# Turning the step's result on VectorE: 32x32 blocks out of PSUM in place of two TensorE transposes

## The chip, the cores and the metric

The kernel runs on one core of one Trainium2 chip. Times are device microseconds (us) of that core. A profiled execution gives a span (first to last instruction) and a trace, and its own time is a little longer than the span.

## The reference, cut to what matters

Two independent layers are put side by side. Layer B is a long convolution; the change touches none of its arithmetic. Layer A is an attention that carries a small memory from one segment of 32 rows to the next, 64 segments (steps) in sequence:

```python
for s in range(n_seg):                                   # 64 steps
    h = concatenate([mem, x[s*32:(s+1)*32]])             # 8 memory rows + 32 rows, 1024 columns
    q, k, v = h @ Wq, h @ Wk, h @ Wv                     # 1024 -> 32 heads x 128
    p = softmax(where(mask, q @ k.T * 128**-0.5, -1e9))
    o = (p @ v) @ Wo                                     # back to 1024 columns
    mem = o[:8]                                          # the only link to the next step
    outs.append(o[8:])
```

So a step can't begin its projections of the memory rows before the step in front has its result `o`. All weights together are 32 MB in bfloat16, and not all of them stay on chip.

## The kernel before, in words

The first 700 us or so hold layer B and, woven into it, what of layer A does not depend on the memory: x is transposed (`Ahead.transposes`, L93), and the keys and queries (`PKd`) and values (`VXd`) of eight rows of each segment are computed ahead and parked in DRAM (`Ahead.projections`, L115). Then `part_a` (L233) runs the 64 steps one after another, under an order of instructions that is written out by hand: each engine executes its instructions in the order of the program text, and only semaphores tie the engines together.

One step, from L478 on. `hT` is the step's input, already transposed: 128 partitions, 8 chunks of the 1024 columns (`kc`, called keys here when a chunk of a weight is meant), 32 columns, of which 24 are x rows (`XM`) and the last 8 the memory rows. `quads` (L358) does one projection of 16 heads: for each of the eight keys `kc` four matmuls, one for each quarter of TensorE's columns, with `hT[:, kc, :]` as stationary operand. The step goes: k of half 0, q of half 0, part of k of half 1, transposes of k and q (`tr`), scores of half 0 (`scores`, L387), and so on through q, v, softmax, and the output projection (`oproj`, L468), which sums into `pp[:, 1, :]` in PSUM: 128 partitions x 256 float32, where partition 32*qt+r holds row r and columns 256*qt to 256*qt+255.

Weights come from three places. Most stay on chip. Twelve of the 64 blocks of a step (512 KB each) are streamed from DRAM copies `WD` into four rotating buffers `wst`; the SP queue issues a load (`stage`, L294) as soon as TensorE has finished with the buffer. Three blocks are kept in PSUM (`KEPT`, L29) and are copied by VectorE into a shared scratch tile just before use: `fetch` (L311) makes five copies (L292) for key 7 of k, whose last piece goes to the tile `a_S`.

The scratch tile `arena` is one block of bytes with hand-given places (`AT`, L36). The place `ob` (byte 4960, 1024 bytes) holds the step's result on its way out; the place `pk` (byte 0) holds the parked keys and queries of the step. `load_pk` (L325) is issued on ScalarE's queue; `put_kl` (L378) is GpSimd's copy (L379) from it into the tile `KT0`, which the first score matmul (L390) needs.

The end of a step before the change, L564 to L584, in the order of each engine:

- TensorE: the output projection; the five small matmuls for `pl` (L444, L448); two 128x128 transposes of the result, `tro` (L574); then key 0 of the next step.
- ScalarE: two copies of `pp[:, 1]` to `osb`, the first half of `ob` (L568); copy L579; the issue of `load_pk` for the next step (L581, its trace line is L327); copy L582; the issues of two stores (L343, L347).
- VectorE: two copies from `tro` into the memory columns of `hT` (L576); then the five copies of `fetch`.

The first projection of a step takes its keys in the order 0, 2, 4, 6, 1, 3, 5, 7, because the first L576 fills the even chunks and the second the odd ones. The GpSimd copy `put_xt` (L336) has filled the x columns of `hT` long before.

Of the kernel before, what the change touches and what calls it, by code (L numbers as in the profile page):

```python
# [10 lines left out]
BF16 = mybir.dt.bfloat16  # L11
F32 = mybir.dt.float32
# [27 lines left out]


def weight_blocks(Wq, Wk, Wv, Wo):
    W3 = {"k": Wk.rearrange("(kc p) he -> kc p he", p=128),
          "q": Wq.rearrange("(kc p) he -> kc p he", p=128),
          "v": Wv.rearrange("(kc p) he -> kc p he", p=128)}
    WoU = Wo.rearrange("(u h e) d -> u e h d", h=2, e=128)

    def src(key):
        if isinstance(key, str):
            return W3[key]  # L50
        if key[0] == "o":
            return WoU[key[1]]
        m, t, kc = key
        return W3[m][kc][:, t * 2048:(t + 1) * 2048]
    return src
# [18 lines left out]
class Ahead:  # L74
# [18 lines left out]
    def transposes(self, pool, ps, ident):  # L93
        nc = self.nc
        def load(b):
            xb = pool.tile([128, self.Dm], BF16, name="xb", tag="xb")
            nc.gpsimd.dma_start(out=xb[:], in_=self.x[b * 128:(b + 1) * 128, :])
            return xb
        xbs = [load(b) for b in range(3)]
        yield  # L100
        for b in range(self.S // 128):
            if b + 3 < self.S // 128:
                xbs.append(load(b + 3))
            xb = xbs[b]
            pt = ps.tile([128, self.KC, 4, self.SL], BF16, name="pt_x", tag="ptx")
            for kc in range(self.KC):
                nc.tensor.transpose(out=pt[:, kc, :, :].rearrange("p a b -> p (a b)"), in_=xb[:, kc * 128:(kc + 1) * 128], identity=ident[:])
            yield
            xst = pool.tile([128, 4, self.KC, self.XM], BF16, name="xst", tag="xst")
            nc.scalar.copy(out=xst[:].rearrange("p s k r -> p k s r"), in_=pt[:, :, :, 0:self.XM])  # L110
            nc.scalar.copy(out=self.xTl[:, :, 4 * b:4 * b + 4, :], in_=pt[:, :, :, self.XM:self.SL])  # L111
            nc.sync.dma_start(out=self.VXd[4 * b:4 * b + 4, :, 256:].rearrange("s p f -> p s f"), in_=xst[:].rearrange("p s k r -> p s (k r)"))
            yield
# [119 lines left out]
def part_a(ctx, tc, x, src, WD, HE, seg_len, out_a, ahead, W_res, rest, places, first):  # L233
    nc = tc.nc
    S, Dm = x.shape
    M = 8
    SL = seg_len
    E = 128
    KC = Dm // 128
    NS = S // SL  # L240
    assert SL == 32 and M == 8 and Dm == 1024 and HE == 4096
    XM = 24
# [114 lines left out]
    for s in range(NS):  # L357
        def quads(m, t, kcs, a=None):  # L358
            if a is None:
                a = ps.tile([128, 512], F32, name="acc", tag=BANK[m, t])  # L360
            for kc in kcs:
                w = unit((m, t, kc))
                for g in range(4):
                    for o_, rhs in columns(w, 512 * g, 512):
                        nc.tensor.matmul(a[32 * g:32 * g + 32, o_:o_ + rhs.shape[1]], lhsT=hT[:, kc, :], rhs=rhs,  # L365
                                         start=(kc == 0), stop=(kc == KC - 1), tile_position=(0, 32 * g), skip_group_check=True)
            return a
# [107 lines left out]
                            nc.tensor.matmul(po[32 * qt:32 * qt + 32, o_:o_ + rhs.shape[1]], lhsT=oT[:, h % 4, (h % 16) // 4, :], rhs=rhs,  # L475
                                             start=False, stop=(h == 31), tile_position=(0, 32 * qt), skip_group_check=True)

        a = quads("k", 0, (0, 2, 4, 6, 1, 3, 5, 7))  # L478
        k0 = evac(a, "k0")
        a = quads("q", 0, range(0, 6))  # L480
        fetch(("q", 0, 7))
# [82 lines left out]
        oproj(pp[:, 1, :], (8, 10, 12, 14, 9, 11, 13, 15), o1)  # L564
        ob = at("ob", 2, 256)
        osb = ob[:, 0, :]
        for j in range(2):
            nc.scalar.copy(out=osb[:, 128 * j:128 * j + 128], in_=pp[:, 1, 128 * j:128 * j + 128])  # L568
        pl = ps.tile([128, 4, 32], F32, name="pl", tag="b2")
        pv_l(pl[:], 1, V1, L1)  # L570
        if s + 1 < NS:
            pt_o = [ps.tile([128, 4, SL], BF16, name="tro", tag=tag) for tag in ("b0", "b1")]
            for j in range(2):
                nc.tensor.transpose(out=pt_o[j][:].rearrange("p a b -> p (a b)"), in_=osb[:, 128 * j:128 * j + 128], identity=ident[:])  # L574
            for j in range(2):
                nc.vector.tensor_copy(out=hT[:, :, XM:SL].rearrange("p (q j) r -> p j q r", j=2)[:, j], in_=pt_o[j][:, :, XM:SL])  # L576
        if s + 1 < NS:
            fetch(("k", 0, 7))
        nc.scalar.copy(out=ob[:, 1, 0:128], in_=pp[:, 0, 0:128])  # L579
# [815 lines left out]
@with_exitstack  # L1395
def kernel(
    ctx: ExitStack,
    tc: tile.TileContext,
    A_x: bass.AP,
    A_mem0: bass.AP,  # L1400
    A_Wq: bass.AP,
    A_Wk: bass.AP,
    A_Wv: bass.AP,
    A_Wo: bass.AP,
    A_seg_len: bass.AP,
    B_u: bass.AP,
    B_A_re: bass.AP,
    B_A_im: bass.AP,
    B_B_re: bass.AP,
    B_B_im: bass.AP,  # L1410
    B_C_re: bass.AP,
    B_C_im: bass.AP,
    B_log_dt: bass.AP,
    B_Dskip: bass.AP,
    out: bass.AP,
):
    seg_len = int(A_seg_len)
    Dm = A_x.shape[2]
    Db = B_u.shape[2]
    out_a = out[0, :, 0:Dm]  # L1420
    out_b = out[0, :, Dm:Dm + Db]
    src = weight_blocks(A_Wq.rearrange("d h e -> d (h e)"), A_Wk.rearrange("d h e -> d (h e)"),
                        A_Wv.rearrange("d h e -> d (h e)"), A_Wo.rearrange("h e d -> (h e) d"))
    WD, copies = streamed_copies(ctx, tc, src)
    ahead = Ahead(ctx, tc, A_x[0], src, seg_len)
    ctx_w = ctx.enter_context(ExitStack())
    W_res, places, first = {}, [], {}
    rest = Keys(RESIDENT)
    rest.ctx = ahead.ctx = ctx_w

    def residents(stay, early):
        def put(t_):
            load_resident(tc, None, src, rest.pop(0), W_res, None, t_)
        for _ in range(EARLY[0]):
            load_resident(tc, stay, src, rest.pop(0), W_res)
            yield
        four = ahead.pool.tile([128, 4, 2048], BF16, name="W4", tag="kst")
        for t_ in [four[:, i, :] for i in range(4)]:
            put(t_)
            yield  # L1440
        for n in range(2):
            for t_ in early[0:6] if n == 0 else early[6:8]:
                put(t_)
                yield
            two = stay.tile([128, 2, 2048], BF16, name="W2", tag="KT%d" % n)
            for i in range(2):
                put(two[:, i, :])
                yield
        two = ahead.pool.tile([128, 2, 2048], BF16, name="W2", tag="xTl")
        for i in range(2):  # L1450
            put(two[:, i, :])
            yield
        for _ in range(4):
            put(ahead.pool.tile([128, 2048], BF16, name="W1", tag="wsl", bufs=4))
            yield
        ahead.wst = ctx_w.enter_context(tc.tile_pool(name="a_wst", bufs=1, side="right"))
        pool = ctx_w.enter_context(tc.tile_pool(name="a_wre0", bufs=1, side="right"))
        for _ in range(EARLY[1]):
            load_resident(tc, pool, src, rest.pop(0), W_res)
            yield  # L1460
        for i, key in enumerate([("k", 0, 7)] + streamed_keys()[0:SLOTS - 1]):
            first[key] = t_ = ahead.wst.tile([128, 2048], BF16, name="wst", tag="w%d" % i)
            tc.nc.sync.dma_start(out=t_[:], in_=WD[key][:] if key in WD else src(key))
            yield
        for i in range(8):
            places.append(lambda i=i: stay.tile([128, 2048], BF16, name="W1", tag="MI%d" % i))
        for i in range(LATE):
            put(places.pop(0)())
            yield

    low = low_blocks(ctx, tc)
    ahead.low = low.pop()
    copies += [lambda t_=t_: load_resident(tc, None, src, rest.pop(0), W_res, None, t_) for t_ in low]

    def first_state(m0, xt):
        nc = tc.nc
        hT = constants(tc, ahead)
        nc.sync.dma_start(out=xt[:].rearrange("p k r -> p (k r)"), in_=ahead.VXd[0, :, 256:])
        nc.sync.dma_start(out=m0[:], in_=A_mem0[0])
        pm = yield  # L1480
        for kc in range(8):
            nc.tensor.transpose(out=pm[:, kc, :], in_=m0[:, kc * 128:(kc + 1) * 128], identity=ahead.consts[0][0:8, 0:8])
        nc.vector.tensor_copy(out=hT[:, :, ahead.XM:], in_=pm)
        nc.gpsimd.tensor_copy(out=hT[:, :, 0:ahead.XM], in_=xt[:])
        yield

    with ExitStack() as ctx_b:
        part_b(ctx_b, tc, B_u[0], B_A_re, B_A_im, B_B_re, B_B_im, B_C_re, B_C_im, B_log_dt, B_Dskip, out_b, ahead, copies, residents, first_state)
    with ExitStack() as ctx_a:
        part_a(ctx_a, tc, A_x[0], src, WD, A_Wo.shape[0] * A_Wo.shape[1], seg_len, out_a, ahead, W_res, rest, places, first)  # L1490
# [35 lines left out]
```

## Time and profile before

| | us |
|---|---|
| median of 3 runs | 2073.23 |
| lowest and highest of them | 2067.98, 2073.27 |
| profiled execution, its own time | 2060.34 |
| its span | 2058.6 |
| of it: PE, DVE, ACT busy | 1875.7, 1416.1, 1051.5 |
| first and last L576, that is the 63 boundaries between steps | 749.3, 1976.7 |
| mean granted TensorE clock | 0.982 |

PE is TensorE's matmul side and PEld its weight loads, DVE is VectorE, ACT ScalarE, POOL GpSimd and SP the engine whose queue issues most DMAs. An ending q (ACTq, SPq) marks what an engine's queue does itself, such as issuing a DMA. In a line of the timeline the first column is the start in the span, the second the duration; then come engine, line of the kernel, operation, output<-input and count, and in brackets how long the engine had been idle and what released it. L390 is line 390 of the kernel before. From L579 on, the changed kernel has the same lines two numbers lower.

### The profile page before, as it was taken

To read this page: it belongs to the slowest core of one execution; us is meant where nothing else is said; L and a number is where in the kernel's file an instruction comes from. 1 tells how busy PE (TensorE), PEld (TensorE's weight loads), DVE (VectorE), ACT (ScalarE), POOL (GpSimd) and SP (SyncE) were. 2 spreads that over 40 slices of the span, in tenths; PEclk is the share of its full clock that TensorE was granted. 3 is DMA by queue.
4 is the path that set the end of the run, shared out by engine and by line. 5 is a ranking of instruction groups with operands and counts; after the bars stand their busy time and mean duration, and the time that the engine had idled before them with its cause. 6 is when DMAs were issued, how large, how long until landed. Compare 5 with 4: busy or idle time off the path is not lost.

```text
span 2058.6 us, 78592 instructions
## 1 busy us (share of the span) xinstructions
PE 1875.7 (91%) x33734; PEld 1190.4 (58%) x33734; DVE 1416.1 (69%) x3352; ACT 1051.5 (51%) x1981; POOL 379.8 (18%) x748
## 2 busy tenths in 40 slices
PE   2699999977999779999999999999999999999999
PEld 1365666656888535555555555555555555555554
DVE  8689989989899346666656656666566666666650
ACT  5899999961333234444444444444444444444430
POOL 2133343353000011111111111111111111111121
PEclk9999999989999879999999999999999999999999
DMA  7697986565736899999999999999999999999991
GB/s 192 177 255 213 261 229 180 157 207 184 228 123 206 311 330 340 341 342 344 344 334 340 340 339 339 347 333 334 338 340 354 344 343 347 339 331 350 333 341 52
DMA packets 351186, 590.78 MB, mean 287 GB/s; under 512 B 108536, under 2 KB 228376, under 8 KB 348788
## 3 DMA queue, kind: packets, MB, share of 16 engines
q1 hardware_dynamic: 297016, 528.00, 75.6%
q10 hardware_dynamic: 44812, 28.26, 4.4%
q0 software_dynamic: 9008, 29.49, 4.3%
q8 instruction: 264, 4.33, 0.8%
q14 instruction: 86, 0.70, 0.1%
HBM read 530.86 MB, written 65.26 MB: 290 GB/s over the span
## 4 chain that ended last, share of the span: by engine, by line
PE 35%; DMA 17%; DVE 1%; issue 1%; ACT 1%; POOL 0%; ACTq 0%; POOLq 0%; DVEq 0%
PE acc L365 20%; PE pp L475 7%; DMA wst<-WD_v 4%; DMA wst<-WD_o 4%; DMA wst<-WD_q 3%; PE pe L611 3%; DMA wst<-WD_k 3%; DMA arena<-PKd 2%; PE tr L376 2%; PE pv L444 1%; DMA out_dram<-arena 1%; PE sc L390 1%; PE pv L448 1%; ACT arena L568 0%; PE sc L394 0%
## 5 line engine op out<-in xcount | busy, mean ns | idle before, releaser
L365 PEld LDWEIGHTS <-a_hT 128*32 128x32 bf16 x12352 | 338.6, 96 | 305.9 <-issue 59.2
L371 ACT CAST arena<-acc 128x512 bf16<-128x512 f32 x384 | 225.1, 586 | 377.0 <-PE acc L365 315.9
L365 PE MATMUL acc<-W,a_hT 128*32 128x512 bf16 x4608 | 375.8, 383 | 0.8 <-issue 0.7
L475 PEld LDWEIGHTS <-arena 128*32 128x32 bf16 x8256 | 212.1, 97 | 93.9 <-issue 45.3
L365 PE MATMUL acc<-wst,a_hT 128*32 128x512 bf16 x2304 | 234.1, 383 | 19.2 <-DMA wst<-WD_v 10.0
L292 DVE TENSOR_SCALAR arena<-keep 128x256 int32<-128x256 int32 (+1 forms) x512 | 176.4, 396 | 42.1 <-PE acc L365 38.0
L379 POOL COPY arena<-arena 128x128 bf16<-128x128 bf16 x128 | 37.6, 294 | 854.1 <-DMA arena<-PKd 316.5
L365 PE MATMUL acc<-MF,a_hT 128*32 128x512 bf16 x2048 | 172.6, 384 | 0.0
L475 PE MATMUL pp<-W_o,arena 128*32 128x256 bf16 x4096 | 138.2, 275 | 7.7 <-DMA W_o<-in_A_Wo_dram 6.3
L414 DVE TENSOR_REDUCE a_mx<-sc 128x4 f32<-128x160 f32 (+1 forms) x192 | 73.1, 381 | 81.8 <-ACT sc L410 81.8
L406 DVE TENSOR_REDUCE a_mx<-sc 128x4 f32<-128x160 f32 (+1 forms) x192 | 72.0, 375 | 82.3 <-PE sc L394 80.6
L167 PE MATMUL pro<-xTl,wsl 128*128 128x512 bf16 x512 | 119.0, 383 | 9.5 <-ACT xTl L111 5.0
L410 ACT ACTIVATE sc<-sc 128x160 f32<-128x160 f32 (+1 forms) x192 | 63.9, 333 | 120.6 <-DVE sc L407 101.3
L1060 PEld LDWEIGHTS <-MF 128*128 128x128 bf16 x1024 | 102.6, 101 | 30.2 <-issue 8.7
L490 DVE COPY arena<-tr 128x512 bf16<-128x512 bf16 x64 | 27.2, 425 | 130.7 <-PE tr L376 130.7
L437 POOL TENSOR_TENSOR arena<-arena,a_BD 128x128 bf16<-128x128 bf16 x128 | 71.1, 555 | 240.1 <-DVE arena L424 221.0
L1060 PE MATMUL hps<-KT,MF 128*128 128x256 bf16 x720 | 94.6, 284 | 14.4 <-DVE x L1229 11.3
L461 ACT CAST arena<-pv 128x256 bf16<-128x256 f32 (+1 forms) x192 | 79.1, 449 | 49.0 <-PE pp L444 39.1
L1287 PE MATMUL yp<-Bt,MI 128*128 128x256 bf16 x680 | 102.9, 273 | 0.8 <-ACT yb L1303 0.8
L568 ACT CAST arena<-pp 128x128 bf16<-128x128 f32 x128 | 27.8, 269 | 141.7 <-PE pp L475 141.7
L1098 ACT ACTIVATE E<-pa 128x648 bf16<-128x648 f32 x128 | 91.4, 714 | 16.9 <-PE pa L1090 9.4
L365 PE MATMUL acc<-W_v,a_hT 128*32 128x512 bf16 x1280 | 93.7, 382 | 0.9 <-issue 0.8
(313 smaller groups left out, 3966.6 us busy)
## 6 DMA issues: line engine op xcount, KB each, us to landing
wst<-WD_v SPq DMA_DIRECT2D x256, 512.0 KB
wst<-WD_k SPq DMA_DIRECT2D x192, 512.0 KB
wst<-WD_o SPq DMA_DIRECT2D x192, 512.0 KB
wst<-WD_q SPq DMA_DIRECT2D x128, 512.0 KB
Ud<-ux POOLq DMA_DIRECT2D x16, 1024.0 KB, 5.5
uq<-Ud SPq DMA_DIRECT2D x32, 512.0 KB
wsl<-in_A_Wk_dram SPq DMA_DIRECT2D x16, 512.0 KB
wsl<-in_A_Wv_dram SPq DMA_DIRECT2D x16, 512.0 KB
```

Source lines behind the costliest of these rows:

```text
L167: nc.tensor.matmul(a[:], lhsT=w[:, kc, 128 * j:128 * j + 128], rhs=xTl[:, kc, :, :].rearrange("p s k -> p (s k)"), start=(kc == 0), stop=( ...
L292: nc.vector.tensor_scalar(out=out.bitcast(I32), in0=in_.bitcast(I32), scalar1=0, scalar2=None, op0=ALU.bitwise_or)
L365: nc.tensor.matmul(a[32 * g:32 * g + 32, o_:o_ + rhs.shape[1]], lhsT=hT[:, kc, :], rhs=rhs, start=(kc == 0), stop=(kc == KC - 1), tile_pos ...
L371: nc.scalar.copy(out=q, in_=a[:])
L406: nc.vector.tensor_reduce(out=m_, in_=x, axis=AX.X, op=ALU.max)
L414: nc.vector.tensor_reduce(out=m_, in_=x, axis=AX.X, op=ALU.add)
L437: nc.gpsimd.tensor_tensor(out=L[:, 0].rearrange("p (a b) k -> p a b k", a=4), in0=bc(lt[:, :, 0:XL].unsqueeze(2), [128, 4, 4, XL]), in1=bc ...
L461: nc.scalar.copy(out=o[:, i:i + n], in_=p[:, i:i + n, :].rearrange("p a (g q) -> p a g q", g=4))
L475: nc.tensor.matmul(po[32 * qt:32 * qt + 32, o_:o_ + rhs.shape[1]], lhsT=oT[:, h % 4, (h % 16) // 4, :], rhs=rhs, start=False, stop=(h == 3 ...
L1060: pe.matmul(s_[r][half][:, cs, :], lhsT=MF[:, kc, 4 * rr + mc, cs, :], rhs=rhs, start=(i == 0 and mc == 0), stop=(i == 1 and mc == 3), ski ...
L1098: sc.activation(out=T["E", r, e // 4][:, lo:lo + 8 * NE].rearrange("p (i c) -> p i c", i=2), in_=T.pop(("p", r, e))[:, :, 0:4 * NE], func= ...
L1287: pe.matmul(yp[:, b, :], lhsT=m_[:, b, cs, kc, :], rhs=Bt[:, kc, j, half, c_, :], start=(kc == 0 and cs == 0 and half == 0), stop=(kc == 3 ...
```

## The change

Column 8*p+k of the 1024 is now in chunk k at partition p, in place of column 128*k+p. So the weights' rows, the columns of x and those of the first memory are given to the partitions by eights. With that arrangement a 32x32 block transpose of `pp[:, 1, :]`, taken with a step of eight columns, lands where `hT` wants it without crossing from one group of 32 partitions to another. VectorE does it straight from PSUM into `hm`, a float32 tile of 1024 bytes that lies at the place `ob`, and copies its memory columns to `hT`, first chunks 0 and 1, then 2 to 7. The two TensorE transposes and ScalarE's two copies in front of them go; one ScalarE copy of the whole result to `osb`, for the store, stands behind. The first projection takes its keys in the order 0 to 7.

```diff
-    W3 = {"k": Wk.rearrange("(kc p) he -> kc p he", p=128),
+    W3 = {"k": Wk.rearrange("(p kc) he -> kc p he", p=128),
...
-                nc.tensor.transpose(out=pt[:, kc, :, :].rearrange("p a b -> p (a b)"), in_=xb[:, kc * 128:(kc + 1) * 128], identity=ident[:])
+                nc.tensor.transpose(out=pt[:, kc, :, :].rearrange("p a b -> p (a b)"), in_=xb[:].rearrange("r (p k) -> r k p", p=128)[:, kc, :], identity=ident[:])
...
-        a = quads("k", 0, (0, 2, 4, 6, 1, 3, 5, 7))
+        a = quads("k", 0, range(KC))
...
         osb = ob[:, 0, :]
-        for j in range(2):
-            nc.scalar.copy(out=osb[:, 128 * j:128 * j + 128], in_=pp[:, 1, 128 * j:128 * j + 128])
+        if s + 1 < NS:
+            hm = at("ob", 512).bitcast(F32).rearrange("p (k r) -> p k r", r=SL)
+            for k in (slice(0, 2), slice(2, KC)):
+                nc.vector.transpose(out=hm[:, k, :], in_=pp[:, 1, :].rearrange("p (d k) -> p k d", k=KC)[:, k, :])
+                nc.vector.tensor_copy(out=hT[:, k, XM:SL], in_=hm[:, k, XM:SL])
         pl = ps.tile([128, 4, 32], F32, name="pl", tag="b2")
         pv_l(pl[:], 1, V1, L1)
-        if s + 1 < NS:
-            pt_o = [ps.tile([128, 4, SL], BF16, name="tro", tag=tag) for tag in ("b0", "b1")]
-            for j in range(2):
-                nc.tensor.transpose(out=pt_o[j][:].rearrange("p a b -> p (a b)"), in_=osb[:, 128 * j:128 * j + 128], identity=ident[:])
-            for j in range(2):
-                nc.vector.tensor_copy(out=hT[:, :, XM:SL].rearrange("p (q j) r -> p j q r", j=2)[:, j], in_=pt_o[j][:, :, XM:SL])
+        nc.scalar.copy(out=osb, in_=pp[:, 1, :])
```

The same re-spacing is made for the q and v weights and for the eight transposes of the first memory (L1482).

More of the change, by code (lines that the diff above doesn't have):

```diff
@@ L42, in weight_blocks @@
 def weight_blocks(Wq, Wk, Wv, Wo):
-    W3 = {"k": Wk.rearrange("(kc p) he -> kc p he", p=128),
-          "q": Wq.rearrange("(kc p) he -> kc p he", p=128),
-          "v": Wv.rearrange("(kc p) he -> kc p he", p=128)}
+    W3 = {"k": Wk.rearrange("(p kc) he -> kc p he", p=128),
+          "q": Wq.rearrange("(p kc) he -> kc p he", p=128),
+          "v": Wv.rearrange("(p kc) he -> kc p he", p=128)}
     WoU = Wo.rearrange("(u h e) d -> u e h d", h=2, e=128)
@@ L1481, in first_state @@
         for kc in range(8):
-            nc.tensor.transpose(out=pm[:, kc, :], in_=m0[:, kc * 128:(kc + 1) * 128], identity=ahead.consts[0][0:8, 0:8])
+            nc.tensor.transpose(out=pm[:, kc, :], in_=m0[:].rearrange("r (p k) -> r k p", p=128)[:, kc, :], identity=ahead.consts[0][0:8, 0:8])
         nc.vector.tensor_copy(out=hT[:, :, ahead.XM:], in_=pm)
```

## The prediction

> **What bounds the kernel now.** I read the 40 slices first. The 64 steps fill the slices from the 14th on, and there two things are nearly full at once:
>
> ```profile
> PE   2699999977999779999999999999999999999999
> ...
> DMA  7697986565736899999999999999999999999991
> ```
>
> TensorE and DMA both show 9 throughout. I call E the end of a step's last output-projection matmul. Between the first E and the last of the 63 with a step behind them (748.57 and 1975.93) a step takes 19.80 us in the mean. The quickest, undisturbed, take 19.08, so about 0.7 us a step are waits. The windows view gives the DMA engines a share of 0.93 to 0.97 here.
>
> Next the waits, to see which are long and who has them:
>
> ```profile
> POOL arena L379 <- DMA arena<-PKd: 316.5, 47, 8.0
> ...
> PEld L365 <- DVE a_hT L576: 14.9, 63, 0.3
> ...
> PE acc L365 <- DMA wst<-WD_v: 10.0, 16, 2.0
> ```
>
> (After the colon: us in total, times, longest.) The wait that the change touches is the second row, 14.9 us in 63 boundaries, and the chain in front of it. TensorE's own waits for streamed blocks are small (10.0 here; 5.9, 2.1 and 6.7 in the rows of k, q and o: 24.7 us in all). The longest is GpSimd's, L379, for the load of `pk`, in 47 of 64 steps. GpSimd's idle time matters only if TensorE stands behind it, so I went to the timeline of one boundary (E = 1915.21 + 0.22 = 1915.43):
>
> ```profile
> 1915.21 0.22 PE L475 MATMUL pp<-a_S,arena 128*32 128x128 bf16 x1
> ...
> 1915.52 0.27 ACT L568 CAST arena<-pp 128x128 bf16<-128x128 f32 x1 [1.87 <-PE pp L475]
> 1915.58 0.33 ACTq L327 DMA_DIRECT2D arena<-PKd  x1
> 1915.68 0.27 ACT L568 CAST arena<-pp 128x128 bf16<-128x128 f32 x1
> 1915.83 0.26 PEld L574 LDWEIGHTS <-arena 128*128 128x128 bf16 x2 [0.28 <-ACT arena L568]
> ...
> 1916.10 0.34 DVE L576 COPY a_hT<-tro 128x32 bf16<-128x32 bf16 x2 [1.37 <-PE tro L574]
> ...
> 1916.33 3.56 PEld L365 LDWEIGHTS <-a_hT 128*32 128x32 bf16 x70 [0.24 <-DVE a_hT L576]
> ...
> 1916.38 1.35 DVE L292 TENSOR_SCALAR arena<-keep 128x256 int32<-128x256 int32 x4
> ...
> 1922.54 0.09 PEld L390 LDWEIGHTS <-arena 128*32 128x32 bf16 x1 [0.19 <-ACT arena L491]
> 1922.87 0.29 POOL L379 COPY arena<-arena 128x128 bf16<-128x128 bf16 x1 [8.01 <-DMA arena<-PKd]
> 1923.21 0.28 PE L390 MATMUL sc<-arena 128*32 128x40 bf16 x16 [0.37 <-POOL arena L379]
> ```
>
> Two things are to be seen. From E to the next step's first weight load are 0.90 us (0.85 in most steps). And the `pk` load, issued 0.15 us behind E, lands 7.3 us later; GpSimd's copy ends at 1923.16, and the first score matmul starts 0.05 behind it, although its weights have been loaded since 1922.54. Step by step through the trace: issue at E+0.10 to E+0.18, from issue to GpSimd's start 4.91 to 7.29 us, mean 6.19; and in 37 of the 63 steps the first score matmul starts exactly 0.05 us behind the end of L379. **So the next step's start is set at E, but its scores are already set by when `pk` is issued.**
>
> **The boundary, what goes and what comes.** Gone: one ScalarE copy ahead (269 ns), TensorE transpose (229 to 230), one VectorE copy (175), with the hops E to first key 0.85. New, on VectorE, free by then:
> - 32x32 transposes of 64 and of 192 float32. No row has float32 from PSUM in steps of eight columns. The nearest are L424 with 64 bf16 from the scratch tile, 203 ns, and L423 with 128, 312, and 256, 445: 192 lies between, 378. That float32 and PSUM need not cost more is shown by L414, which reads 160 float32 of PSUM in 325 ns. Ends: 170 and 310 (the rows for 32 and 128) below; double, 406 and 756, if the step or the type costs two passes. I take 203 and 378.
> - copies of 16 and 48 elements: 175 each, as L576 with 32; L415 with 4 elements is no cheaper (178).
>
> With 0.03 us to start, 0.03 a hop between a transposing and its copy, and the second transpose directly behind the first copy: first copy ends at E+0.44, second at E+1.02. Key 0 can begin at E+0.49 (0.05 behind, as now), 0.36 earlier than today; key 2 at E+1.07, where two keys of 0.215 would have ended at E+0.92.
>
> **But the gain stops at key 7.** `fetch` follows on VectorE: today it starts at E+0.90 in the quick step of E = 1857.39, its last piece ends at E+2.38, and TensorE's matmul on `a_S` starts at E+2.54. Its first copy overlaps the copy in front by 0.07, so behind the new chain it starts at E+0.95 to E+1.02 and ends at E+2.43 to E+2.50: `a_S` can't start before E+2.48 to E+2.55. The front gains 0.06 at most, whatever key 0 does; with the low ends (chain end E+0.92) 0.16. Key 2's streamed block being used one place later, and the keys' order, are worth nothing by themselves.
>
> **The move on ScalarE.** `hm` lies on the bytes of `ob`, so the new copy to `osb` can't start before the second VectorE copy has read `hm`. Queued behind it on ScalarE, in order: copy L579, the issue of `load_pk`, copy L582, two stores. Today the issue leaves 0.06 us behind the first L568 copy's start, at E+0.10 in the median. Now that copy starts at E+1.02+0.03 = E+1.05, the issue leaves at E+1.11: **1.0 us later** (low ends 0.9; doubled transposes 1.6). The stores, then k's eviction (today E+2.9) may slip up to 0.7; the k transposes that use it start at E+5.06, so this is covered.
>
> The price: in each step, scores start at the later of what they have today and L379's end + 1.0 + 0.05. Summed over the 63 steps as they stand in the trace, that is 49.7 us: 37 steps pay the full 1.0 and the others what their 0.08 to 1.5 us of slack leave. (0.85 later: 41; 1.2: 61; 1.6: 85.) TensorE has nothing to do meanwhile, as the scores are next in its order. An earlier key 0 only makes this wait longer.
>
> What comes back: while TensorE pauses, streamed blocks keep landing. Steps whose scores already start late (E+7.2 or more) need 12.80 us from there to the next E, the mean is 12.90. So some 0.13 us a step, 63 times, 8 us; the limit is the 24.7 of waits for streamed blocks. I take 10.
>
> By the Trainium skill, "VectorE: DVE Perf Modes", Rules for kernel authors, a chain on VectorE should have few operations, since the pipe drains after each; it speaks against two operations becoming four. The trace agrees in that the 16 or 32 element rows cost 170 to 175 ns nearly whatever their size. The errata section of that page prices a PSUM read at 120 cycles plus one an element at 0.96 GHz, an estimate of 192 and 325 ns for the two transposes. By it the chain would be 0.06 shorter and the sum 3 us smaller; that is an estimate too.
>
> By "DMA: Bandwidth & Descriptors", Queues, rings and completion order, each DMA engine takes turns between queues packet by packet. If so, `pk` shortens when the streamed queue runs dry; no row here shows it dry. By it the sum could lose some of its 50.
>
> **The first 700 us.** The 128 transposes of x read their columns in steps of eight: no row shows such a weight load. Today's take 147 ns, and the stretch (11.8 to 59.0 us) has 41.1 us of waits for x and 25.5 for ScalarE; doubled they add 19 us, inside those. The q, k and v rows come from addresses farther apart, with pieces of the same sizes: nothing, with 5 us either way for the range. In the profile's last step ScalarE's copies differ by 0.1 us: nothing.
>
> Sum: +49.7 - 10 = +40. On the profiled execution's 2060.3 this gives 2100; I set it on the median of the runs, 2073.2, which is 0.6% above: **2113**.
>
> **Rivals.**
> - Double-cost transposes (chance 0.12): +85 and the same 10 back, 2148. For: strided float32 from PSUM is in no row. Against: L414.
> - The DMA takes it up (0.13): the pause lets the streamed queue run dry around the scores, and `pk` lands 0.8 to 1.0 us sooner behind its issue, 2070 to 2085. For: 4.91 us have been seen. Against: after a step with late scores the next latency is no shorter (5.4 to 6.9 us). About half of this is within 0.3% of before.
> - Faster (0.10): `pk`'s latency falls by more than 1.0 us, so the scores wait for TensorE's own front; today's waits of TensorE for L379 go (7 us over the 63 steps, from the same reading), the low ends' 0.16 a step is left (10), and the first stage may add 5: -6 to -22, 2051 to 2067. It decides if L379 ends before TensorE reaches the scores (E+6.3). That the change doesn't shorten the front is inside the forecast.
>
> **Numbers.** Forecast 0.65 (2087 to 2139: 44 from 0.9 us, with 25 back and 5 from the first stage, up to 61 from 1.2 us, nothing back and 5). A difference under 0.3%, 6 us, can't be told from none. Slower 0.65 + 0.12 + 0.06 = 0.83, same 0.07, faster 0.10. The range 2070 to 2145 leaves out the faster case and the upper half of the doubled one.
>
> **To look for afterwards.** ACTq L327 about 1.1 us behind E (right) or still 0.1; PE L390 released by POOL L379 in nearly all steps, at E+7.7; StreamTranspose of 192 near 0.38; first key at E+0.5 with a stop before key 2; `a_S` at E+2.55. I am wrong if `pk`'s time from issue to L379 falls to some 5 us.

## The result, and the profile after

The changed kernel takes 2086.87 us in the median of 12 runs (2079.54 to 2095.11). Beside them on the same chip, the kernel before takes 2072.22 (12 runs, 2057.52 to 2082.38). The ratio is 1.0085, with a 95% interval of 1.0063 to 1.0106: **slower by 14.65 us, where +40 was forecast.** The profiled execution after has a span of 2085.4 and a time of its own of 2087.16. The profiled one of before, 2060.34, lay 12 us under its median, so the two profiles differ by 26.8.

Measured from E to E as in the prediction, the profiles' 26.8 us divide so: the first E comes 4.3 us sooner (748.57, now 744.25), the 62 periods behind it are 19.80 us and now 20.29, together +30.8, and the rest is +0.3. The loss is in the loop. The 40 slices of the page of after say so only by what they don't show:

```profile
span 2085.4 us, 78464 instructions
...
PE   2699999978999789989999999999999999999999
...
DMA  7686985665646999999999989999999999999991
```

Both rows are as full as before. A wait of half a us in each 20 us doesn't change a tenth. The list of waits of after has it (columns as before: us in total, times, longest):

```profile
POOL arena L379 <- DMA arena<-PKd: 340.4, 47, 8.9
...
PEld L365 <- DVE a_hT L571: 49.8, 120, 0.5
...
PE sc L390 <- POOL arena L379: 28.8, 44, 2.5
...
PE acc L365 <- DMA wst<-WD_v: 8.3, 11, 2.3
```

In the same list of before, the third row was this:

```profile
PE sc L390 <- POOL arena L379: 0.6, 2, 0.4
```

TensorE now stands before the scores, behind GpSimd's copy of `pk`, 44 times and for 28.8 us, nearly the whole loss. The view counts only stretches in which TensorE's records leave it idle; by start and end, the scores start 0.05 us behind L379 in 37 of the 63 boundaries of before and in 53 of after. The second row, 120 waits where there were 63, is the chain in two pieces. The boundary of after with E = 1881.63 + 0.22 = 1881.85 shows both (two stretches of the timeline):

```profile
1881.47 0.32 SPq L297 DMA_DIRECT2D wst<-WD_k  x1
1881.63 0.22 PE L475 MATMUL pp<-a_S,arena 128*32 128x128 bf16 x1
...
1881.88 0.25 DVE L570 STREAM_TRANSPOSE arena<-pp 128x64 f32<-128x64 f32 x1 [0.31 <-PE pp L475]
...
1882.17 0.17 DVE L571 CAST a_hT<-arena 128x16 bf16<-128x16 f32 x1
1882.25 0.38 DVE L570 STREAM_TRANSPOSE arena<-pp 128x192 f32<-128x192 f32 x1
1882.40 0.12 PEld L365 LDWEIGHTS <-a_hT 128*32 128x32 bf16 x8 [0.43 <-DVE a_hT L571]
...
1882.66 0.19 DVE L571 CAST a_hT<-arena 128x48 bf16<-128x48 f32 x1
...
1882.94 0.37 ACT L574 CAST arena<-pp 128x256 bf16<-128x256 f32 x1 [3.01 <-DVE a_hT L571]
1883.04 0.33 ACTq L327 DMA_DIRECT2D arena<-PKd  x1
```

```profile
1888.15 0.09 PEld L390 LDWEIGHTS <-arena 128*32 128x32 bf16 x1 [0.19 <-ACT arena L491]
...
1889.25 0.29 POOL L379 COPY arena<-arena 128x128 bf16<-128x128 bf16 x1 [7.54 <-DMA arena<-PKd]
1889.59 0.28 PE L390 MATMUL sc<-arena 128*32 128x40 bf16 x16 [1.13 <-POOL arena L379]
```

Key 0 starts at E+0.55. ScalarE's copy L574 starts behind the end of VectorE's second copy L571, and the `pk` load behind it is issued at E+1.19, 1.57 us behind the streamed block's issue in the first row. L379 ends at E+7.69, and the score matmul starts 0.05 behind it, its weights having been loaded since 1888.24. That block's issue on SP's queue is to matter more than I thought. In the boundary of before that the prediction shows (`pk` issued at 1915.58) it stood only 0.32 us ahead:

```profile
1915.26 0.32 SPq L297 DMA_DIRECT2D wst<-WD_k  x1
```

Over the 63 boundaries, worked out step by step from the trace (medians in the first two rows, as a few boundaries that wait for a block start far later; means in the others):

| from E, us | before | after | change |
|---|---|---|---|
| first key, median | 0.85 | 0.55 | -0.30 |
| matmul on `a_S`, median | 2.59 | 2.49 | -0.10 |
| `pk` issue | 0.12 | 1.21 | +1.09 |
| from that issue to L379's start | 6.19 | 5.67 | **-0.52** |
| end of L379 | 6.61 | 7.17 | +0.56 |
| first score matmul | 6.89 | 7.36 | +0.47 |
| from there to the next E | 12.90 | 12.94 | +0.04 |

The issue is as late as forecast, but half of that came back before the load had landed. My theory was then: the loss is all in the late issue of `pk`, and something shortens a late load. The experiments ask first whether the issue is all, and then what shortens the load.

### The profile page after: what moved, and what is told of

Its sections match the earlier page's. It is cut to its first block, busy times and chain, and to the rows that moved or that the text cites. A ratio compares the mean times of both kernels' runs of the same rounds, so it can differ in the third digit from the quotient of the medians.

```text
span 2085.4 us, 78464 instructions
## 1 busy us (share of the span) xinstructions
PE 1865.5 (89%) x33608; PEld 1194.9 (57%) x33608; DVE 1448.9 (69%) x3478; ACT 1048.8 (50%) x1917; POOL 378.2 (18%) x748
## 5 line engine op out<-in xcount | busy, mean ns | idle before, releaser
L365 PEld LDWEIGHTS <-a_hT 128*32 128x32 bf16 x12352 | 357.0, 96 | 299.2 <-issue 54.9
L365 PE MATMUL acc<-W,a_hT 128*32 128x512 bf16 x4608 | 380.5, 383 | 1.7 <-issue 1.7
L475 PEld LDWEIGHTS <-arena 128*32 128x32 bf16 x8256 | 210.1, 96 | 95.0 <-ACT arena L461 43.7
L365 PE MATMUL acc<-wst,a_hT 128*32 128x512 bf16 x2304 | 238.4, 382 | 15.0 <-DMA wst<-WD_v 8.3
L292 DVE TENSOR_SCALAR arena<-keep 128x256 int32<-128x256 int32 (+1 forms) x512 | 176.3, 395 | 30.3 <-PE acc L365 24.7
L379 POOL COPY arena<-arena 128x128 bf16<-128x128 bf16 x128 | 37.5, 293 | 872.3 <-DMA arena<-PKd 340.4
L365 PE MATMUL acc<-MF,a_hT 128*32 128x512 bf16 x2048 | 176.9, 381 | 0.0
L475 PE MATMUL pp<-W_o,arena 128*32 128x256 bf16 x4096 | 137.7, 275 | 5.5 <-DMA W_o<-in_A_Wo_dram 5.4
L574 ACT CAST arena<-pp 128x256 bf16<-128x256 f32 x64 | 23.8, 372 | 204.3 <-DVE a_hT L571 202.4
L1096 ACT ACTIVATE E<-pa 128x648 bf16<-128x648 f32 x128 | 91.4, 714 | 17.4 <-PE pa L1088 10.5
```

Of the source, the lines that this page charges most:

```text
L292: nc.vector.tensor_scalar(out=out.bitcast(I32), in0=in_.bitcast(I32), scalar1=0, scalar2=None, op0=ALU.bitwise_or)
L1096: sc.activation(out=T["E", r, e // 4][:, lo:lo + 8 * NE].rearrange("p (i c) -> p i c", i=2), in_=T.pop(("p", r, e))[:, :, 0:4 * NE], func= ...
```

## The experiments

"Issue" is the mean time of `pk`'s issue from E, "landing" the mean from there to the start of L379's copy, "scores" the mean of the first score matmul from E, "tail" the mean from there to the next E; "waits" are TensorE's waits for streamed blocks, in all. Medians are of timed runs; ratios are to the kernel before on the same chip. For before these five columns are 0.12, 6.19, 6.89, 12.90 and 24.7; for after 1.21, 5.67, 7.36, 12.94 and 20.1.

### The issue of pk alone

`e1_after_pk_first` is the changed kernel with the load issued ahead of the copy that waits:

```diff
+        if s + 1 < NS:
+            pk = load_pk(s + 1)
         nc.scalar.copy(out=osb, in_=pp[:, 1, :])
...
-        if s + 1 < NS:
-            pk = load_pk(s + 1)
```

> The changed kernel with one line moved: the issue of the pk load stands ahead of ScalarE's copy to osb, so it no longer waits for VectorE's second copy. Theory P (the time is lost because pk is issued 1.1 us later behind E, and the scores wait for it): the issue goes from E+1.20 to about E-0.05, the first score matmul from E+7.36 in the mean to 6.65 to 6.80; over 63 steps 35 to 45 us below the changed kernel's profile, ratio to the kernel before 0.992 to 0.998. Rival W (the price is elsewhere: the farther addresses of the weights, four VectorE operations for two, later stores): the ratio stays at 1.006 to 1.011. Rival D (the DMA queues set the length of a step, whatever pk does): 1.000 to 1.005.

`e2_before_pk_late` is the kernel before with the load moved between the two stores of `stores`, behind the one to `OLd`:

```diff
         nc.scalar.dma_start(out=OLd[s // 8][...], in_=ob[:, 1, :])
+        if s + 1 < NS:
+            load_pk(s + 1)
...
-        if s + 1 < NS:
-            pk = load_pk(s + 1)
```

> The kernel before with its own TensorE transposes and layout, only the issue of the pk load moved behind the first of the two stores on ScalarE's queue, to about E+1.18 in place of E+0.10. Theory P: it loses what the change loses, ratio 1.006 to 1.014, with pk's time from issue to GpSimd's copy falling from 6.2 to about 5.7 us as in the changed kernel. If that time stayed at 6.2, as the prediction had it: 1.020 to 1.025. Rival W: 0.998 to 1.002, as none of the change's parts is in it.

`e3_before_pk_early` and `e4_after_pk_early` split the load into halves. The first half, which L379 reads, is issued 2.6 us ahead of E (median), the second where the whole load was; for this the tile `ln1`, which lay on those bytes, moves:

```diff
-      "lb1": 4960, "ln1": 0, ...
+      "lb1": 4960, "ln1": 3072, ...
...
         o1 = evac_o(pv1, "o1", 2)
+        if s + 1 < NS:
+            load_pk(s + 1, 0)
```

> The kernel before with the pk load in two halves: the half that the first scores need is issued 2.4 us ahead of E, behind ScalarE's second o1 copy (its place in the scratch tile is made free by putting ln1 where pn1 was), the other half where the whole was. Theory P: it lands at about E+3.5, the scores wait for TensorE's own front alone, in the median at E+6.5; the 7 us of waits for L379 that the profile before holds go, ratio 0.993 to 0.998. Rival D: 1.000, the waits come back at the streamed blocks.

> The same early half of pk in the changed kernel. Theory P: with pk out of the way the change shows its own worth, which is the earlier matmul on a_S (E+2.49 for E+2.55, 63 times 0.06 = 4 us): ratio to the kernel before 0.990 to 0.997, and 0 to 6 us below the kernel before with the early half. Rival W: above it, by up to 15 us.

| | median | ratio [95%] | issue | landing | scores | tail | waits |
|---|---|---|---|---|---|---|---|
| e1 | 2065.46 | 0.9986 [0.9963, 1.0010] | -0.42 | 6.41 | 6.84 | 13.07 | 34.9 |
| e2 | 2116.72 | 1.0231 [1.0197, 1.0264] | 1.29 | 6.03 | 7.77 | 12.77 | 18.5 |
| e3 | 2064.76 | 0.9975 [0.9947, 1.0003] | early | | 6.76 | 13.06 | 36.6 |
| e4 | 2057.08 | 0.9957 [0.9933, 0.9980] | early | | 6.79 | 12.98 | 30.9 |

In e1 the changed kernel, with all its new parts but with the load ahead, is as fast as before, and little is left of the 28.8 us before the scores:

```profile
PE sc L390 <- POOL arena L379: 4.0, 6, 2.0
```

The ratio is a little above the 0.992 to 0.998 that I expected. So the loss is the late issue, and the transposes on VectorE, the new order of keys and the arrangement by eights cost nothing that these runs can tell from none. (The mean issue of -0.42 holds one boundary in which `pk` went out over 10 us ahead; the median is -0.10. So it is in e13 and e14 below, with medians of -0.10 and -0.32.)

But e2 missed. Issued only 0.08 us later than in after, `pk` landed 0.36 us slower than there, and the loss was more than twice as big. The waits of e2 for the scores (there L392 and L381):

```profile
PE sc L392 <- POOL arena L381: 54.9, 52, 2.3
```

54.9 us, where after has 28.8. So when `pk` is issued doesn't alone say when it lands; what was issued just before it may count too. In e2 that is the store to `OLd`, 0.42 us ahead in the same queue.

The early halves gain little: the scores start 0.1 us sooner, and TensorE's waits for streamed blocks rise from 24.7 to 36.6 and 30.9 us. Those of e4:

```profile
PE acc L366 <- DMA wst<-WD_v: 11.6, 14, 2.4
...
PE pp L476 <- DMA wst<-WD_o: 9.4, 15, 1.0
PE acc L366 <- DMA wst<-WD_k: 8.2, 13, 1.5
...
PE acc L366 <- DMA wst<-WD_q: 1.7, 3, 0.6
```

### Later without the store, and a shorter chain

`e5_before_pk_late_clear` puts the late issue into the kernel before without moving it past any DMA: VectorE clears two elements of `pk` behind its L576 copies, and the load has to wait for that. Nothing else of the change is in it.

```diff
+            nc.vector.memset(at("pk", 2), 0.0)
```

> The kernel before, pk's issue held back to about E+1.1 as in the changed kernel and, as there, ahead of both stores: VectorE clears two elements of pk's place behind its second L576 copy, and the load waits for that (one VectorE operation of some 0.1 us is added ahead of fetch). Theory G (what pk pays from issue to its first packet depends on what was issued just ahead: a streamed block 0.3 to 0.5 us ahead in the kernel before, 1.4 to 1.6 us ahead in the changed kernel, a store 0.4 us ahead in the run with pk late): the first packet comes 1.7 to 1.9 us behind the issue, GpSimd's copy 5.5 to 5.8 behind it, the scores at E+7.3 to E+7.45, ratio 1.007 to 1.015. Rival (the time from issue to landing is near its 6.0 to 6.2 us and only the changed kernel's own parts shorten it): 1.020 to 1.025.

`e6_after_pk_later` is the edit of e2 in the changed kernel, so that the issue is late twice.

> The changed kernel with pk's issue one more place later, behind the first store, at about E+2.2. Theory G: the discount is used up, the streamed block is far ahead already, so the whole further microsecond is paid: scores at E+8.2 to E+8.5, ratio to the kernel before 1.025 to 1.045. Rival (pk lands quicker the later it is issued because the streamed queue runs dry while TensorE waits): scores at E+7.8 or earlier, ratio under 1.020.

`e7_after_one_turn` does the turn in one transpose and one copy; `e8_after_one_turn_early` adds the early half of e4.

```diff
-            for k in (slice(0, 2), slice(2, KC)):
+            for k in (slice(0, KC),):
```

> The changed kernel with one transpose of 256 and one copy of 64 in place of the two pairs. From the rows of the changed kernel (0.25 for 64, 0.38 for 192, copies 0.17 and 0.19) the chain ends at E+0.70 in place of E+1.01: key 0 starts at E+0.75 in place of E+0.55, pk is issued at E+0.88 in place of E+1.20. Theory P with G: some 0.1 of the 0.3 us is lost again behind the streamed block, scores 0.15 to 0.25 earlier than in the changed kernel, ratio to the kernel before 1.003 to 1.007. Rival (key 0 sets the step, as the change supposes): 0.2 us a step worse than the changed kernel, ratio 1.012 to 1.016.

> One transpose and one copy, with the early half of pk. The scores wait for TensorE alone, so the front counts: fetch ends at about E+2.1, a_S is then limited by TensorE at E+2.43 (E+2.49 with two pairs). Theory F (the front sets the step once pk is out of the way): 2 to 6 us below the kernel with two pairs and the early half, ratio to the kernel before 0.991 to 0.996. Theory D (streamed blocks give a step its floor of some 19.7 us, so nothing more is to be had): the same as with two pairs, 0.994 to 0.998.

| | median | ratio [95%] | issue | landing | scores | tail | waits |
|---|---|---|---|---|---|---|---|
| e5 | 2086.43 | 1.0098 [1.0079, 1.0118] | 1.09 | 5.57 | 7.19 | 12.99 | 31.9 |
| e6 | 2149.42 | 1.0402 [1.0370, 1.0433] | 2.29 | 5.77 | 8.41 | 12.95 | 10.5 |
| e7 | 2061.94 | 0.9986 [0.9964, 1.0008] | 0.93 | 5.38 | 6.86 | 12.96 | 31.3 |
| e8 | 2055.13 | 0.9960 [0.9943, 0.9977] | early | | 6.76 | 13.00 | 33.7 |

e5 repeats the loss of the change, 1.0098 beside 1.0085, with none of its parts, and a landing 0.62 us shorter than before. Its waits for the scores:

```profile
PE sc L390 <- POOL arena L379: 17.0, 28, 1.8
```

e6 speaks against the rival of the prediction by which the pause of TensorE lets the streamed queue run dry. Its pause is far longer, and the load lands no sooner than in after (5.77 against 5.67): 1.08 us of issue cost 1.05 us of scores. The first 1.1 us of delay brought back half, the next 1.1 brought nothing. The traces say it directly: from `pk`'s issue to L379 the DMA engines are busy for 97% of the time in before, in after and in e6, and in no boundary of the three is there a moment without a streamed block on its way.

e7 gained more than expected. Its boundary with E = 1520.27 + 0.22 = 1520.49:

```profile
1520.11 0.32 SPq L297 DMA_DIRECT2D wst<-WD_k  x1
...
1520.53 0.45 DVE L570 STREAM_TRANSPOSE arena<-pp 128x256 f32<-128x256 f32 x1 [0.31 <-PE pp L475]
...
1521.01 0.19 DVE L571 CAST a_hT<-arena 128x64 bf16<-128x64 f32 x1
...
1521.40 0.33 ACTq L327 DMA_DIRECT2D arena<-PKd  x1
```

One transpose of 256 takes 0.45 us, the two of 64 and 192 take 0.25 + 0.38; one copy 0.19, two 0.17 + 0.19. The chain ends at E+0.71 in place of E+1.00, and the issue is 0.28 us sooner in the mean. The scores are 0.5 us sooner, more than that, since `pk` also lands in 5.38. In the waits of e7 little is left of the 28.8:

```profile
PE sc L390 <- POOL arena L379: 4.7, 10, 0.9
```

Key 0 starts later than in after (E+0.77 in this boundary), and that costs nothing, as `a_S` comes at E+2.46 to E+2.51 in most boundaries all the same.

e8 and e4 end at the same place, and so nearly do e1, e3, e7 and before: periods of 19.76 to 19.90 us. **Below that the streamed blocks seem to hold a step** (theory D): what the scores gain, the waits for blocks take back. This is argued from the waits, in one profile each, and the profile of before, with its 24.7, was a quick one. No run streams fewer blocks, and the 2 to 6 us by which theory F would set e8 under e4 are no more than the width of the two intervals.

### What shortens a late load

From the packets in the trace, I took when `pk`'s first packet starts. Before: 2.77 us behind the issue (median); after: 1.72. The rest of the way, first packet to last, got longer (in the mean 2.69, then 3.18); the two together are the 0.5 us that came back. What differs is how far `pk` is issued behind the last streamed block: 0.40 us before, 1.57 after. The two numbers sum to 3.17 and 3.29. Theory G: **in the median, the first packet of `pk` starts some 3.3 us behind the issue of the streamed block ahead of it, whenever `pk` itself is issued in between.** Then a delay of `pk` is free as long as it eats into that time. Its rival is that `pk`'s place after E decides, by what else runs there.

`e9_before_pk_mid` moves the load in the kernel before one copy further back (behind L582, ahead of the stores):

```diff
-        if s + 1 < NS:
-            pk = load_pk(s + 1)
         nc.scalar.copy(out=ob[:, 1, 128:256], in_=pl[:]...)
+        if s + 1 < NS:
+            pk = load_pk(s + 1)
```

> The kernel before with the issue of pk one instruction later on ScalarE's queue, behind the copy of pl, still ahead of the stores: at about E+0.5 in place of E+0.10. Theory G (pk's first packet comes no sooner than some 3 us behind the streamed block issued at about E-0.4, so the first 0.8 us or so of delay are free): GpSimd's copy still ends at E+6.5 to E+6.75, the time from issue to it falls by 0.3 to 0.4, ratio 0.998 to 1.004. Rival (every tenth of a microsecond is paid, as the prediction had it): L379 ends 0.4 later, ratio 1.007 to 1.011.

`e10_before_o13_sooner`, `e11_after_o13_sooner` and `e12_after_one_turn_o13` leave `pk` where it is and use block 13 of the output projection two places sooner, so that its buffer comes free and the next block can be issued sooner:

```diff
-        oproj(pp[:, 1, :], (8, 10, 12, 14, 9, 11, 13, 15), o1)
+        oproj(pp[:, 1, :], (8, 10, 12, 14, 13, 9, 11, 15), o1)
```

> The kernel before with unit 13 of the output projection, the last streamed block of a step, used two places sooner, so that the streamed load which follows in its buffer is issued 0.87 us sooner, at about E-1.25 in place of E-0.4; pk's own issue stays at E+0.10. Theory G: pk's first packet comes 1.8 to 2.2 us behind its issue in place of 2.77, and GpSimd's copy 5.3 to 5.8 behind it in place of 6.19; ratio 0.993 to 1.000. Rival (the block issued just ahead has no part in it): 2.6 to 2.9 and 6.0 to 6.3, ratio 0.999 to 1.003.

> The changed kernel with the same swap. The streamed block is then issued about 2.4 us ahead of pk in place of 1.5. Theory G: the first packet of pk, now 1.77 behind its issue, gains 0.1 to 0.5, the scores come 0.1 to 0.5 sooner, ratio to the kernel before 0.999 to 1.006. Rival: no difference from the changed kernel, 1.006 to 1.011.

> The changed kernel with one transpose and one copy and the same swap, pk issued at about E+0.93. Theory G: the block is 2.1 us ahead, pk's first packet comes 1.5 to 1.9 behind its issue in place of 2.05, the scores 0.1 to 0.3 sooner; but the streamed blocks hold a step at 19.75 to 19.8 us, as in the two kernels with the early half of pk, so ratio 0.994 to 0.999. Rival: 0.998 to 1.000, as without the swap.

At last a pair that keeps `pk`'s place and moves the block from ahead of it to behind it. `e13_before_pk_first` has the load ahead of the two copies L568; `e14_before_pk_first_o13_last` has that and the order (8, 10, 12, 14, 9, 11, 15, 13), with the `stop` mark of the sum's last matmuls moved to unit 13. Each has one timed execution, the profiled one.

> The kernel before with pk's issue ahead of ScalarE's two L568 copies, at E-0.1 or a little sooner; the streamed block in front of it still goes out at about E-0.4. The control of the next run. Theory G: pk's first packet 2.5 to 3.0 us behind its issue, 2.8 to 3.5 behind the block's.

> The same, with unit 13 last in the output projection, behind unit 15, so that the streamed block that takes its buffer goes out at about E+0.05, behind pk's issue and not ahead of it; unit 15 then comes one place sooner than its copy by VectorE is ready, and costs some 0.4 us a step, so the time isn't to be compared, only pk's way. Theory G (pk's first packet waits for the block issued just ahead): the block ahead is now 1.5 us or more older, the first packet comes 1.4 to 2.0 us behind pk's issue. Rival (the place within the step decides, not the block): 2.4 to 3.0 as in the control.

"Gap" is the median from the streamed block's issue to `pk`'s, "first" the median from `pk`'s issue to its first packet, "sum" these two added:

| | median | ratio [95%] | gap | first | sum | issue | landing | scores |
|---|---|---|---|---|---|---|---|---|
| before | | 1 | 0.40 | 2.77 | 3.17 | 0.12 | 6.19 | 6.89 |
| e13 | 2071.08 | one execution, before beside it 2073.72 | 0.28 | 2.62 | 2.90 | -0.49 | 6.42 | 6.89 |
| e9 | 2068.23 | 0.9994 [0.9971, 1.0017] | 0.73 | 2.50 | 3.23 | 0.41 | 5.85 | 6.86 |
| e10 | 2068.50 | 1.0008 [0.9990, 1.0025] | 0.76 | 2.55 | 3.31 | 0.13 | 5.76 | 6.76 |
| e7 | (above) | | 1.26 | 2.03 | 3.28 | 0.93 | 5.38 | 6.86 |
| e5 | (above) | | 1.37 | 1.94 | 3.31 | 1.09 | 5.57 | 7.19 |
| after | 2086.87 | 1.0085 [1.0063, 1.0106] | 1.57 | 1.72 | 3.29 | 1.21 | 5.67 | 7.36 |
| e12 | 2063.81 | 0.9973 [0.9956, 0.9991] | 1.57 | 1.73 | 3.30 | 0.94 | 5.22 | 6.81 |
| e11 | 2079.78 | 1.0076 [1.0047, 1.0105] | 1.85 | 1.59 | 3.44 | 1.22 | 5.60 | 7.28 |
| e14 | 2068.95 | one execution, as e13 | 1.58 | 1.84 | 3.42 | -0.57 | 5.88 | 6.70 |
| e6 | (above) | | 0.75 | 2.54 | 3.29 | 2.29 | 5.77 | 8.41 |

The sum stands at 3.2 to 3.4, 2.9 where `pk` is issued only 0.28 behind, while the issue itself goes from E-0.57 to E+2.29. (Added up in each boundary first, the medians are 3.1 to 3.5 in all eleven. Single boundaries scatter: in before, eight of ten lie between 2.8 and 3.6.) It explains e6 too: there the next streamed block has gone out 0.75 us ahead of `pk`, and the waiting begins anew.

In e9 a delay of 0.29 us costs nothing: the landing is 0.34 shorter. In e10 I missed: the gap grew by only 0.36 us, where the block was to move by 0.87. SP issues it 0.04 us behind the end of unit 13 in both kernels, and two places bring that end only from E-0.33 to E-0.66. The first packet followed it by 0.22 and the scores by 0.13, while the waits for blocks rose to 36.0 and the time stayed. In e11 and e12 the gap grows by 0.3 us each, and the first packet follows by 0.13 and 0.30. The scores come only 0.08 and 0.05 sooner, less than I expected of both, and the ratio of e11, 1.0076, is the one that its rival had: so small a gain at the first packet doesn't show in the time. After and e12 have the same gap and the same first packet, with issues 0.27 us apart from E, and a score start 0.55 apart; the other half of that lies between first and last packet. The pair e13 and e14 tells place from block. (L475 on `a_S` belongs to unit 15; in e14 unit 13 follows it, so E is later than that row.) One boundary of e13:

```profile
1504.92 1.76 SPq L297 DMA_DIRECT2D wst<-WD_k  x2
1506.39 0.22 PE L475 MATMUL pp<-a_S,arena 128*32 128x128 bf16 x1
...
1506.50 0.33 ACTq L327 DMA_DIRECT2D arena<-PKd  x1
...
1513.18 0.29 POOL L379 COPY arena<-arena 128x128 bf16<-128x128 bf16 x1 [6.71 <-DMA arena<-PKd]
```

and the same one of e14:

```profile
1504.14 2.26 SPq L297 DMA_DIRECT2D wst<-WD_k  x2
1505.61 0.22 PE L475 MATMUL pp<-a_S,arena 128*32 128x128 bf16 x1
...
1505.72 0.33 ACTq L327 DMA_DIRECT2D arena<-PKd  x1
...
1511.00 0.29 POOL L379 COPY arena<-arena 128x128 bf16<-128x128 bf16 x1 [5.31 <-DMA arena<-PKd]
```

The first row holds two issues; the second of them starts at the row's end less 0.32, so at 1506.36 in e13, 0.14 ahead of `pk`, and at 1506.08 in e14, 0.36 behind it. At the same place `pk` needs 6.68 us to L379 in the one and 5.28 in the other. In the median the first packet comes at 2.62 and at 1.84. So the block decides, not the place.

Is it the block's issue, or how many blocks are still on their way? When `pk` is issued, these are four in most boundaries of before, e9 and e10, and three in most of e5, e6, e7, after, e11 and e12. With three the first packet still comes anywhere from 1.59 (e11, gap 1.85) to 2.54 us (e6, gap 0.75), and at a gap of 0.73 to 0.76 it comes at 2.50 to 2.55 with three (e6) as with four (e9, e10). So the number of blocks doesn't stand in for the gap. How much of the oldest of them is left shrinks as the gap grows, and no run tells these two apart.

## Why the prediction was wrong

**Right** were the direction and the mechanism. `hm` on the bytes of `ob` holds back ScalarE's copy and with it the issue of `pk`, by 1.09 us (1.0 forecast); TensorE then stands before L390 behind L379. The chain's parts were near: 250 and 375 ns for the transposes (203 and 378 forecast), 174 and 189 for the copies, key 0 at E+0.55 (0.49), `a_S` at E+2.49 (2.48 to 2.55), so the front gained little, as said: 0.10 in the median, 0.06 from the quickest boundaries of before to those of after (2.55, 2.49). By the Trainium skill, "VectorE: DVE Perf Modes", errata section, the estimate was 192 and 325 ns, and for 256 elements it would be 392; the trace's 250, 375 and 450 are 50 to 58 above it, the measurement decides. The same page's advice to keep a chain short in operations agrees with e7, whose ratio is 1% below that of the change.

**The step that failed** is "scores start at the later of what they have today and L379's end + 1.0 + 0.05". It took `pk`'s time from issue to landing in each step as fixed (6.19 us in the mean). That fell to 5.67, and L379's end moved by 0.56. With 0.56 in place of 1.0, the prediction's own reading of the 63 steps gives 24.7 us in place of 49.7, and 29 were measured (63 times 0.465). I had named the sign for this ("falls to some 5 us") and had the low latencies, 4.91, in hand, but asked only whether the queue runs dry, which it doesn't. Part of the 6.19 goes with the streamed block issued 0.40 us ahead, and a later `pk` spends less of it waiting. By the Trainium skill, "DMA: Bandwidth & Descriptors", Issuing engines are not separate DMA queues, DMAs started on different engines run on the same 16 DMA engines and interleave. Here a first packet comes some 3.3 us behind the other queue's block, in the median, so interleaving alone doesn't tell when it starts.

**A smaller miss:** "I take 10" for what comes back from streamed blocks. Their waits fell from 24.7 to 20.1, 4.6, and the tail didn't shorten (12.90, 12.94). That goes against me. The two errors partly cancel, and that is luck: the price was some 20 us too high, the return too high by 5 or more, and the net of the loop was +31 in the profiles where +40 stood.

**The base:** the rest, from +27 between the profiles to +14.65 between medians, is that the profiled execution of before was quick by 12 us. I set the sum on the median all the same, as if a usual execution had the waits of that quick one. So of the 25 us between +40 and +14.65 some 9 are the loop, 4 the first stage, and 12, the largest part, this base. Why that execution was quicker is not settled, nor where a usual one spends the 12 us. Nor is the first stage: 750.1 us to the first E in the mean of eight profiles of the old arrangement (746.2 to 752.8), 747.4 of eight of the new (743.7 to 751.3). They overlap.

**Open** are what makes the 3.3 us (something that follows the block's issue, or what is left to move of the blocks ahead), and why the spread from first to last packet differs, 2.4 to 3.3 us.

**The best versions** are e8 and e4, 0.9960 and 0.9957: the change with `pk`'s first half issued early. They beat the kernel before by 0.4%, with intervals that leave out 1, and no more, as it seems because streamed blocks hold the step.

## What to carry to other kernels

When a copy gets a new wait, count the DMA issues queued behind it on its engine: a load whose tile has nothing to do with the change was the whole loss that these runs can tell, and putting its issue ahead of the waiting copy undid it. A load's latency read from a trace isn't a constant to be moved with its issue; look at what was issued just before it on the other queues, since a delay can use up the part spent behind that, as in e9. And on this short chain one longer operation beat two pairs, though the first half of the result then came later.

## What was unexpected of the hardware

- A 128 KB load issued on ScalarE's queue within 0.3 to 1.9 us behind a 512 KB load on SP's queue, with the DMA engines over 90% busy, has its first packet 2.9 to 3.4 us behind the issue of the large one, going by the medians of eleven kernels.
- With a store issued 0.42 us ahead in the same queue, gap and first packet sum to 3.71 us in e2; in e6, which has the same store ahead but a streamed block closer, to 3.29. So what the store adds is not settled.
- VectorE's 32x32 transpose of float32 out of PSUM in steps of eight columns: 250, 375 and 450 ns for 64, 192 and 256 elements a partition, next to 203 and 445 for 64 and 256 bf16 out of the scratch tile. Neither the type nor the step doubled it.
- The transposes of x with weights read in steps of eight columns load in 167 ns in place of 147 (medians); the stretch's last one starts at 59.0 us in both profiles, so the waits there hide it.
